# One sum of second weights made in place of its block, and three token-tile pairs instead of one in seven block products in the first unit

## The chip, the cores and the metric

The kernel runs on one core of one Trainium2 chip. The metric is the device time of one execution in microseconds. Engines: PE (TensorE, matmuls), DVE (VectorE), ACT (ScalarE), POOL (GpSimd) and SP (SyncE, which only issues transfers here).

## The reference

```python
def _attn_ref(q, k, v):                       # 8 batches, 12 heads, 448 tokens, 64 wide
    scores = scale * np.matmul(q, k.transpose(0, 1, 3, 2))
    attn = np.maximum(scores, 0.0) ** 2 / S
    return np.matmul(attn, v)
...
def _moe_ref(x, g_ln, w_ch1, w_ch2):          # x: 8 x 448 x 768
    mu = np.mean(x, axis=-1, keepdims=True)
    var = np.mean((x - mu) ** 2, axis=-1, keepdims=True)
    xn = (x - mu) / np.sqrt(var + 1e-06) * g_ln
    ch = np.maximum(xn @ w_ch1, 0.0) @ w_ch2  # 768 x 3072, then 3072 x 768
    return x + ch
```

Attention comes first, its heads are put side by side as x, and x goes through the two layers.

## The kernel before

Inputs and output are float32; what TensorE reads is bfloat16. The eight batches follow one another. In each, q and k of a period (four heads, three periods to a batch, numbered through all batches) are loaded by POOL's queue and transposed by a transfer on SP's queue; scores (L610) go through relu (L619 on ACT, L621 on DVE), a square (L634 on DVE, L636 on POOL) and AV (L676). The result, x transposed, is summed (POOL, L767 to L770), centred (save L874, subtraction L882), and goes through the first layer (L970, L988, or in seven block products L1210) to h, which is held as 24 blocks of 128 by tokens.

**Units and tiles.** The second layer takes two batches as a unit u, whose 896 tokens are seven tiles m of 128. In unit 0, tiles 0 to 2 are batch 0, tiles 4 to 6 are batch 1, and tile 3 has a part of each. h of tiles 0 to 3 lies in h1, that of tiles 4 to 6 in hb. The second weight w2 (24 blocks of 128 x 768) is seen as four quarters, b11 and b12 (upper 12 blocks, left and right 384 columns), b21 and b22 (lower 12 blocks).

**Single tiles** (`ffn_2`, L1535): for each half of the columns, 24 matmuls of 128 x 384 into a bank (four steps of six, L1543) and one evacuation (L1559), which multiplies by the row's factor and adds x.

**Pairs in seven products** (`ffn_w`, L1421): two tiles and the four quarters are a 2 x 2 block product that is done in seven products P1, P2, P6, P5, P7, P3, P4 of 12 matmuls each (two steps of six, L1452), with an evacuation after each (L1460). On the side of the weights they need the sums T3 = b22 + b12, T1 = b12 - b11, T2 = T3 - b11, T4 = b21 - T2 (`make_sum`, L1309; 12 blocks of 128 x 384 each, written at L1320, L1322, L1328, L1330); on the side of h the differences S3, S2, S1, S4 (`s_op`, L1397, two instructions each, L1408), S3, S1 and S4 in place and S2 in a block of its own (`s2_of`).

In unit 0 the tiles 4, 5, 6, 3, 2 are single and (0, 1) is a pair; in the other units tile 2 is single and (0, 1), (3, 4), (5, 6) are pairs. `store_tile` issues two transfers for each piece of output.

**Order.** All instructions are ordered by a planner when the program is built (class `Order`): steps are put on the engine lists with estimated costs; on each engine the step that can start first goes first, then the one with the lower key; steps with two engines are given to the one that ends them sooner and yield to steps of one engine that could start at the same time. `segment` places TensorE's work of a stage: it walks through the stage's steps (`f1_steps` of one batch, then steps of the second layer) and puts pieces of the next batch's attention, the visits, between them when they are due and ready; then the next batch is centred. Hooks at numbered steps add other work: the block sums (`next_sum`, key 5.0), the scaling of w1 by g_ln (`put_gains_on_w1`, L1035 on ACT, L1037 on DVE), the differences of a pair (`pair_start`, key -2.9). Evacuations have key -3.0.

The stage that holds unit 0's second layer is built by the call of `segment` at L1820: the first layer of batch 1 (24 steps of six matmuls), five single tiles (40 steps), one pair (14 steps), with batch 2's attention as visits. `make_w1_sums` and `make_x_sums` place the sums for the first layer of later batches.

Of the kernel before, what the change touches and what calls it, by code (L numbers as in the profile page):

```python
# [202 lines left out]
def kernel(  # L203
# [10 lines left out]
    nc = tc.nc  # L214
    P = 128
# [8 lines left out]
    J = 7  # L224
# [830 lines left out]
    D_FREE = J * hd  # L1055
    T3_HOME = slice(D_FREE + 2 * W_BLOCK, D_FREE + 2 * W_BLOCK + KQ * SH)

    def make_w1_sums(first):

        if first:  # L1060
            places = ([("D", D_FREE + i * W_BLOCK, []) for i in range(2)]
                      + [("B", i * W_BLOCK, [later("s2 used", 0)] if i < 2 else []) for i in (2, 3, 4, 5, 6, 0, 1)])
        else:
            places = ([("C", i * W_BLOCK, [later("qk_done", LAST_B)]) for i in range(7)]
                      + [("D", T3_HOME.start, [later("f1_end", LAST_B - 1)]), ("at", 0, [later("av_done", LAST_B)])])
        b_done = 2 if first else LAST_B - 1

        def home(kind, o):
            t = at_all if kind == "at" else region(kind)
            return t[:, o:o + W_BLOCK].rearrange("p (k c) -> p k c", k=KQ)  # L1070
# [35 lines left out]
    def make_x_sums(b):  # L1106
# [10 lines left out]
        else:  # L1117
            o = x_all[:, 4:6, :].rearrange("p m c -> p (m c)")
            t = {"T1": o[:, :n], "T2": o[:, n:2 * n], "T3": region("D")[:, T3_HOME], "T4": homes["v"][:, 2 * RING * S:2 * RING * S + n]}
# [189 lines left out]
    def make_sum(name, k, o, deps, key):  # L1309
# [5 lines left out]
        prev = {"T1": [], "T3": [], "T2": "T3", "T4": "T2"}[name]  # L1315
# [17 lines left out]
        m = n if prev else 1  # L1333
# [6 lines left out]
    def make_sums(part):  # L1340

        if part == 0:
            v_t = v_pool.tile([P, H // 2, S], bf16, tag="v0")
            c_t = xc_pool.tile([P, K1, S], bf16, tag="xc0")
            v_b, c_b = (blocks(t.rearrange("p a c -> p (a c)"), J) for t in (v_t, c_t))
            x_b = blocks(xT_all[:, 4 * d_model:], 6)
            x_free = [ops[x, bb] for x in ("x_read", "turn_x") for bb in range(2)]
            at_end = blocks(at_all[:, (N_AT - 1) * 2 * S:], 5)
            todo = ([("T3", k, v_b[:, k:k + 2], []) for k in (0, 2, 4)] + [("T3", k, c_b[:, k - 6:k - 4], []) for k in (6, 8, 10)]
                    + [("T1", 7 + k, at_end[:, k:min(k + 2, 5)], [later("av_done", 1)]) for k in (0, 2, 4)] + [  # L1350
                    ("T2", 0, v_b[:, 6:7], []), ("T2", 1, c_b[:, 6:7], []),
                    ("T2", 2, x_b[:, 0:2], x_free), ("T2", 4, x_b[:, 2:4], x_free), ("T2", 6, x_b[:, 4:6], x_free)])
        else:
            a_t = big_pool.tile([P, BIG], bf16, tag="A")
            a_b = blocks(a_t, 14)
            d_b = blocks(region("D"), J)
            gone, turned = [ops["f2_end", 1]], [ops["qk_free", 1]]
            todo = ([("T2", k, a_b[:, k - 8:k - 6], gone) for k in (8, 10)]
                    + [("T1", a, d_b[:, a:z], turned) for a, z in ((0, 2), (2, 4), (4, 6), (6, 7))]
                    + [("T4", k, a_b[:, k + 4:k + 6], gone) for k in (0, 2, 4, 6, 8)]  # L1360
                    + [("T4", 10, blocks(x_all[:, 6, :], 2), [later("m2_out")])])
        sum_queue.extend(todo)
# [9 lines left out]
    def s2_of(u):  # L1372

        return region("B")[:, :KH * P].rearrange("p (k c) -> p k c", c=P) if u == 0 else s2_home
# [22 lines left out]
    def s_op(u, m, name, part, deps):  # L1397

        k = slice(part * KH // 2, (part + 1) * KH // 2)
        k_hi = slice(KH + k.start, KH + k.stop)  # L1400
        a1, a2 = tile_cols(u, m), tile_cols(u, m + 1)
        s2_t = s2_of(u)
        a11, a12, a21, a22 = h1[:, k, a1], h1[:, k_hi, a1], h1[:, k, a2], h1[:, k_hi, a2]
        o, i0, i1 = {"S3": (a21, a21, a11), "S2": (s2_t[:, k], a22, a21), "S1": (a11, a11, s2_t[:, k]),
                     "S4": (a12, a12, s2_t[:, k])}[name]

        def emit(eng):
            (nc.vector if eng == "DVE" else nc.gpsimd).tensor_sub(o, i0, i1)  # L1408
        return R.add("DVE", 570.0, emit, deps, key=-2.9, port=True)
# [11 lines left out]
    def ffn_w(u, m, name, part):  # L1421
# [4 lines left out]
        t1, t2 = (0, 1) if m < 3 else (m - 3, m - 2)  # L1426
# [8 lines left out]
        if final and name == "P4":  # L1435
            last_product(u, m, part, e, r2, deps)
            return
        s2_t = s2_of(u)
# [3 lines left out]
        a = {"P1": lambda k: stat(u, m, k), "P2": lambda k: stat(u, m, KH + k), "P6": lambda k: s2_t[:, k],  # L1442
             "P5": lambda k: stat(u, m, k), "P7": lambda k: stat(u, m + 1, k), "P3": lambda k: stat(u, m, KH + k),
             "P4": lambda k: stat(u, m + 1, KH + k)}[name]
# [12 lines left out]
        def evac(key, tile_n, cols, r, more, deps):  # L1457
            def emit(eng):
                o = e["o", 1 if key in ("p5", "C22") else 0][:, cols]
                nc.vector.scalar_tensor_tensor(o, e["ps", bank], r, o if more else xm[u, m + tile_n][:, cols],  # L1460
# [13 lines left out]
        elif name == "P6":  # L1474
            evac("c2", 0, hi, r1, False, [e["c1"], o_done[e["turn"]][1]])
            s2_last = [op, e["S1"], e["S4"]]
            if m == 3:
# [9 lines left out]
        elif name == "P7":  # L1487
            ev = evac("C22", 1, hi, r2, True, [e["p5"]])
            o_done[1 - e["turn"]][1] = store_tile(u, m + 1, hi, ev, False, e["o", 1])
# [4 lines left out]
        else:  # L1494
# [3 lines left out]
            o_done[e["turn"]][0] = store_tile(u, m + 1, lo, ev, False, e["o", 0])  # L1498
            if m == 3:
                ops["m3_out", u] = e["C12"]  # L1500
            elif m == 5 or u == 0:
                now_known(ev, "f2_out", b)
# [384 lines left out]
```

## Time and profile before

| what | us |
|---|---|
| median of 3 runs | 515.39 (515.30 to 516.42) |
| the profiled execution | 515.06 |
| its span on the core | 513.2 |
| PE / DVE / ACT / POOL busy in the span | 500.2 / 389.9 / 225.6 / 177.7 |
| first layer of batch 1, matmuls | 62 to 96.2 (with the end of batch 0's) |
| unit 0's second layer, with visits | 96.2 to 159.4 |
| first layer of batch 2 starts | 160.0 |

Lines such as L1452 are those of the kernel before. A line of a group gives line, engine, operation, output <- inputs, shape, count and durations. A line of a stretch gives the busy time of each engine in it and, in brackets, the count of instructions. Tiles are named without their numbers: `w` is w1 or w2, `t` and `a_t` are big regions of SBUF, `f_ps` the second layer's banks of PSUM. The granted clock of TensorE is 1.00 throughout.

### The profile page before, as it was taken

The page shows a single profiled execution, that of the slowest core. Times are in us where ns is not written, and L with a number is a line of the kernel's source. Part 1 is how long each engine was busy: PE and PEld are TensorE (multiplying, and loading weights), DVE is VectorE, ACT ScalarE, POOL GpSimd, SP SyncE. Part 2 cuts the span into 40 slices and gives each one's busy share as a digit, 9 for nine tenths or more (in the row PEclk, how much of TensorE's full clock was granted, in tenths as well). Part 3 has the DMA queues.
Part 4 walks back from the last instruction along what each step waited for, and adds up shares of the span by engine and source line. Part 5 has one row for each costly group of instructions (what it writes and reads, how often), then busy time and mean ns, then how long its engine had stood idle before and what let it go on. Part 6 is the DMA issues. An engine that isn't in the chain of part 4 may idle for free.

```text
span 513.2 us, 10746 instructions
## 1 busy us (share of the span) xinstructions
PE 500.2 (97%) x4416; PEld 305.9 (60%) x4416; DVE 389.9 (76%) x732; ACT 225.6 (44%) x351; POOL 177.7 (35%) x205
## 2 busy tenths in 40 slices
PE   5899999999999999999999999999999999999997
PEld 3444455555555445677555775567656675579864
DVE  5988647877986979778778698865888688966843
ACT  5977622652303564156530664236731476115300
POOL 7420500425623066536633067233266033200000
PEclk9999999999999999999999999999999999999999
DMA  9999999789798187797387787894789710123022
GB/s 194 197 188 195 202 202 140 73 104 105 107 145 109 36 86 77 120 157 80 31 119 93 109 79 63 126 128 54 70 84 137 129 21 1 47 63 45 2 63 61
DMA packets 145948, 51.88 MB, mean 101 GB/s; under 512 B 123238, under 2 KB 144108, under 8 KB 145900
## 3 DMA queue, kind: packets, MB, share of 16 engines
q0 software_dynamic: 82224, 25.50, 46.9%
q1 hardware_dynamic: 59036, 18.82, 21.6%
q10 hardware_dynamic: 4640, 6.88, 4.6%
q8 instruction: 34, 0.56, 0.4%
q14 instruction: 14, 0.11, 0.1%
HBM read 51.91 MB, written 11.01 MB: 123 GB/s over the span
## 4 chain that ended last, share of the span: by engine, by line
PE 94%; DVE 3%; ACT 1%; DMA 1%; issue 1%; ACTq 0%; DVEq 0%
PE f_ps L1452 26%; PE f_ps L970 19%; PE f_ps L1543 12%; PE f_ps L1210 10%; PE ps L988 7%; PE sc L610 7%; PE ps L676 5%; PE x_ps L1210 2%; PE y_ps L1210 2%; DVE at_all L634 1%; ACT at_all L619 1%; DVE t L387 1%; DMA f<-in_q_dram 1%; PE ps L532 1%; PE f_ps L950 0%
## 5 line engine op out<-in xcount | busy, mean ns | idle before, releaser
L619 ACT ACTIVATE at_all<-sc 128x896 bf16<-128x896 f32 x120 | 105.4, 925 | 101.1 <-PE sc L610 99.8
L970 PE MATMUL f_ps<-a,w 128*128 128x448 bf16 x516 | 101.5, 353 | 0.0
L634 DVE TENSOR_TENSOR at_all<-at_all 128x896 bf16<-128x896 bf16 x154 | 96.8, 660 | 1.9 <-ACT at_all L619 1.9
L1452 PEld LDWEIGHTS <-h 128*128 128x128 bf16 x708 | 68.4, 98 | 47.3 <-issue 2.8
L442 POOL DMA_DIRECT2D v_t<-in_v_dram x36 | 21.5, 603 | 170.2 <-PE sc L610 145.1
L970 PEld LDWEIGHTS <-w 128*128 128x128 bf16 x516 | 48.9, 98 | 48.8 <-issue 5.5
L1452 PE MATMUL f_ps<-w,h 128*128 128x384 bf16 x360 | 62.8, 326 | 0.0
L423 POOL DMA_DIRECT2D t<-in_k_dram x36 | 55.9, 2137 | 0.0
L423 POOL DMA_DIRECT2D t<-in_q_dram x36 | 42.0, 1340 | 39.5 <-DMA t<-t 28.1
L621 DVE TENSOR_SCALAR at_all<-sc 128x896 bf16<-128x896 f32 x39 | 42.4, 1087 | 15.9 <-PE ps L676 8.7
L999 ACT ACTIVATE h<-f_ps 128x448 bf16<-128x448 f32 (+1 forms) x65 | 32.9, 506 | 47.6 <-PE f_ps L970 46.3
L610 PE MATMUL sc<-t 64*64 64x448 bf16 x672 | 49.5, 367 | 2.9 <-DVE t L387 1.5
L1210 PEld LDWEIGHTS <-w 128*128 128x128 bf16 x432 | 41.0, 98 | 5.8 <-issue 2.7
L988 PE MATMUL ps<-a,w 128*128 128x448 bf16 x186 | 40.2, 352 | 0.0
L1543 PE MATMUL f_ps<-w,h 128*128 128x384 bf16 x240 | 40.0, 326 | 0.0
L1236 DVE CUSTOM_DVE_ANT_0 h<-f_ps,o_all 128x448 bf16<-128x448 f32 x32 | 19.5, 619 | 20.3 <-ACT h L999 6.9
L610 PEld LDWEIGHTS <-t 64*64 64x64 bf16 x672 | 18.4, 107 | 26.3 <-issue 17.9
L1460 DVE SCALAR_TENSOR_TENSOR o_all<-f_ps,r_t,x_all 128x384 f32<-128x384 f32 x39 | 23.9, 613 | 12.0 <-PE f_ps L1452 11.9
L1543 PEld LDWEIGHTS <-h 128*128 128x128 bf16 x240 | 23.3, 98 | 15.8 <-issue 0.6
L1210 PEld LDWEIGHTS <-t 128*128 128x128 bf16 x318 | 30.2, 98 | 4.1 <-issue 1.3
L1460 DVE SCALAR_TENSOR_TENSOR o_all<-f_ps,r_t,o_all 128x384 f32<-128x384 f32 x30 | 18.4, 614 | 16.5 <-PE f_ps L1452 16.5
L385 ACT CAST xT_all<-ps 128x768 bf16<-128x768 f32 (+2 forms) x28 | 17.8, 641 | 28.7 <-PE ps L676 17.7
(158 smaller groups left out, 718.4 us busy)
## 6 DMA issues: line engine op xcount, KB each, us to landing
w<-in_moe_w_ch_dram POOLq DMA_DIRECT2D x4, 1152.0 KB, 39.3
out_dram<-o_all ACTq DMA_DIRECT2D x43, 96.0 KB, 2.7
t<-in_q_dram POOLq DMA_DIRECT2D x36, 112.0 KB, 4.0
t<-in_k_dram POOLq DMA_DIRECT2D x36, 112.0 KB, 5.2
v_t<-in_v_dram POOLq DMA_DIRECT2D x36, 112.0 KB, 3.3
out_dram<-o_all SPq DMA_DIRECT2D x35, 96.0 KB, 2.3
w<-in_moe_w_ch_dram POOLq DMA_DIRECT2D x4, 768.0 KB, 19.0
out_dram<-o_all ACTq DMA_DIRECT2D x13, 192.0 KB, 3.0
```

What stands on the lines that cost most here:

```text
L423: nc.gpsimd.dma_start(qk_stage()[half * T:(half + 1) * T, t].rearrange("p j (h d) -> p j h d", d=D), src[b, h0:h0 + 2].rearrange("h (p j) ...
L610: nc.tensor.matmul(sc[rows_of(half), r, :S], turned[rows_of(r), 1, s, rows_of(half)], turned[rows_of(r), 0, :, rows_of(half)], start=True, ...
L619: nc.scalar.activation(attn[n, s], st[0][:, :, :S], Act.Relu, scale=rc2)
L621: nc.vector.tensor_scalar(attn[n, s], st[0][:, :, :S], rc2, 0.0, op0=Alu.mult, op1=Alu.max)
L634: nc.vector.tensor_mul(attn[n, s], attn[n, s], attn[n, s])
L970: nc.tensor.matmul(st[0], w1[:, ki, ni * P:(ni + 1) * P], xc[b][:, ki, :], start=(i == 0), stop=(i == K1 - 1))
L988: nc.tensor.matmul(st[0], w1[:, ki, ni * P:(ni + 1) * P], xc[b][:, ki, :], start=ki == 0, stop=ki == K1 - 1)
L999: nc.scalar.activation(o, st[0][:, c], Act.Relu)
L1210: nc.tensor.matmul(e["ps", bank][:, n, :], a[:, k, n * P:(n + 1) * P], x[:, k, :], start=name in ("P1", "P2", "P5") and n == 0 and k == 0, ...
L1452: nc.tensor.matmul(e["ps", bank], a(k), w(k), start=new and k == 0, stop=k == KH - 1, skip_group_check=True)
L1460: nc.vector.scalar_tensor_tensor(o, e["ps", bank], r, o if more else xm[u, m + tile_n][:, cols], op0=Alu.mult, op1=Alu.add)
L1543: nc.tensor.matmul(o_st["ps"], stat(u, m, ki), w2[:, ki, j * hd:(j + 1) * hd], start=(ki == 0), stop=(ki == K2 - 1))
```

## The change

- T1 is written over b12 (after T3 has been made from it), not into 12 blocks elsewhere. All sums are queued by one function, two per step from step 13 on. The places of T2 and T4 are others.
- A single tile, which can no longer read b12, is done by way of T1 (`ffn_x`): X = h_up b11 (12 matmuls) is evacuated to the right half with x added; Z = h_up T1 + h_low b22 (24) is added to it; Y = h_low b21 (12) is accumulated on X and evacuated to the left half. Three evacuations in place of two, and two stores in place of one. This holds for tile 2 in all four units.
- In unit 0 the tiles (4, 5) and (6, 3) become pairs in seven products beside (0, 1). The order is: tile 2, (0, 1), (4, 5), (6, 3).
- S2 of unit 0 has another place in two halves; the sums of w1 for the first layer lie in regions A and B, free after pair (6, 3), and partly in C.
- The second of each two stores of unit 0 is issued by SP and not by ACT, as in the other units.

The diff, cut to its core:

```diff
     def make_w1_sums(first):
 
-        if first:
...
+        gone = [ops["f2_end", 1]]
+        places = ([("B", i * W_BLOCK, gone) for i in range(7)] + [("A", i * W_BLOCK, gone) for i in range(7)]
+                  + [("end", W_BLOCK, [later("s2 used", 0)])])
+        n = 3 * G_STEADY
+        places = places[:n] if first else (
+            places[n:] + [("C", i * W_BLOCK, [later("qk_done", LAST_B)]) for i in range(7)] + [("at", 0, [later("av_done", LAST_B)])])
...
-            t = {"T1": o[:, :n], "T2": o[:, n:2 * n], "T3": region("D")[:, T3_HOME], "T4": homes["v"][:, 2 * RING * S:2 * RING * S + n]}
+            t = {"T1": o[:, :n], "T2": o[:, n:2 * n], "T3": x_all[:, 6, :n], "T4": homes["v"][:, 2 * RING * S:2 * RING * S + n]}
...
-        prev = {"T1": [], "T3": [], "T2": "T3", "T4": "T2"}[name]
+        prev = {"T1": "T3", "T3": None, "T2": "T3", "T4": "T2"}[name]
...
-    def make_sums(part):
...
+    AT_END = at_all[:, (N_AT - 1) * 2 * S:]
+
+    def make_sums():
...
+        d_b, d_free = blocks(region("D"), 14), [ops["qk_free", 1]]
+        sum_queue.extend(
+            [("T3", k, v_b[:, k:k + 2], []) for k in (0, 2, 4)] + [("T3", k, c_b[:, k - 6:k - 4], []) for k in (6, 8, 10)]
+            + [("T1", k, b12[:, k:k + 2], []) for k in range(0, KH, 2)]
+            + [("T2", 0, v_b[:, 6:7], []), ("T2", 1, c_b[:, 6:7], [])]
+            + [("T2", k, x_b[:, k - 2:k], x_free) for k in (2, 4, 6)]
+            + [("T2", k, d_b[:, k - 8:k - 6], d_free) for k in (8, 10)]
+            + [("T4", k, d_b[:, k + 4:k + 6], d_free) for k in (0, 2, 4, 6, 8)]
+            + [("T4", 10, blocks(AT_END, 2), [later("av_done", 1)])])
...
-    def s2_of(u):
-
-        return region("B")[:, :KH * P].rearrange("p (k c) -> p k c", c=P) if u == 0 else s2_home
+    def s2_of(u, part):
+
+        if u == 0:
+            t = AT_END[:, W_BLOCK:2 * W_BLOCK] if part else homes["v"][:, 2 * RING * S:2 * RING * S + W_BLOCK]
+            return t.rearrange("p (k c) -> p k c", c=P)
+        return s2_home[:, part * KH // 2:(part + 1) * KH // 2]
+
+    def partner(u, m):
+        return 3 if (u, m) == (0, 6) else m + 1
+
+    def h_block(u, m, upper, part):
+
+        k = slice(part * KH // 2, (part + 1) * KH // 2)
+        if u == 0 and m > 3:
+            return hb[upper][:, k, (m - 4) * P:(m - 3) * P]
+        return h1[:, upper * KH + k.start:upper * KH + k.stop, tile_cols(u, m)]
...
-        k = slice(part * KH // 2, (part + 1) * KH // 2)
-        k_hi = slice(KH + k.start, KH + k.stop)
-        a1, a2 = tile_cols(u, m), tile_cols(u, m + 1)
-        s2_t = s2_of(u)
-        a11, a12, a21, a22 = h1[:, k, a1], h1[:, k_hi, a1], h1[:, k, a2], h1[:, k_hi, a2]
-        o, i0, i1 = {"S3": (a21, a21, a11), "S2": (s2_t[:, k], a22, a21), "S1": (a11, a11, s2_t[:, k]),
-                     "S4": (a12, a12, s2_t[:, k])}[name]
+        s2_t = s2_of(u, part)
+        a11, a12, a21, a22 = (h_block(u, t, upper, part) for t in (m, partner(u, m)) for upper in range(2))
+        o, i0, i1 = {"S3": (a21, a21, a11), "S2": (s2_t, a22, a21), "S1": (a11, a11, s2_t), "S4": (a12, a12, s2_t)}[name]
...
+            if u == 0 and m < 6:
+                now_known(s2_last, "s2_free", 0, 4 if m == 0 else 6)
+            elif m == 3:
...
-            if m == 3:
-                ops["m3_out", u] = e["C12"]
-            elif m == 5 or u == 0:
+            o_done[e["turn"]][0] = store_tile(u, m2, lo, ev, False, e["o", 0])
+            if 3 in (m, m2):
+                ops["m3_out", u] = e["C12"] if m == 3 else ev
+            if (u, m) == (0, 6):
+                ops["f2_end", 1] = op
+            if m in (5, 6) or (u, m) == (0, 0):
...
-    def f2_deps(u, m, j, part, parts):
...
-    def ffn_2(u, m, j, part, parts):
...
+    def fx_deps(u, m, name, part):
+
+        b = 2 * u
+        e = xs.get((u, m), {})
+        a, z = part * KH // 2, (part + 1) * KH // 2
+        if name == "X":
+            return [h_of(b, a, z), min(f_banks, key=when), ops["w2", K2 - 1]]
+        if name == "Z" and part < 2:
+            return [h_of(b, a, z), e["z0"], ops["sums", "T1"]]
+        return [h_of(b, KH, K2)] + ([e["x hi"]] if name == "Y" else [])
+
+    xs = {}
+
+    def ffn_x(u, m, name, part):
+
+        b = 2 * u
+        e = xs.setdefault((u, m), {})
+        deps = fx_deps(u, m, name, part)
+        if name == "X" and part == 0:
+            if when(f_banks[0]) > when(f_banks[1]):
+                f_banks.reverse()
+                f_tags.reverse()
+            e["z0"] = f_banks[1]
+            e["turn"] = o_take()
+        w = b21 if name == "Y" else b11 if name == "X" else b12 if part < 2 else b22
+        upper = name == "Y" or part > 1
+
         def emit(eng):
-            if part == 0:
+            if name in "XZ" and part == 0:
                 o_ps = f_tile([P, hd], fp32)
-                o_st["ps"] = o_ps
-            for ki in range(part * K2 // parts, (part + 1) * K2 // parts):
-                nc.tensor.matmul(o_st["ps"], stat(u, m, ki), w2[:, ki, j * hd:(j + 1) * hd],
-                                 start=(ki == 0), stop=(ki == K2 - 1))
-        op = R.pe(975.0 * 4 / parts, emit, f2_deps(u, m, j, part, parts))
-        if (u, m) == (0, 6) and j == 1 and part == parts - 1:
-            ops["f2_end", 1] = op
-        if part < parts - 1:
-            return
-        ps = o_st["ps"]
-        ri = m if m < 3 else m - 3
-
-        if j == 0:
-            o_st[u, m] = o_take()
-        turn = o_st[u, m]
-
-        def evac(eng):
-            cols = slice(j * hd, (j + 1) * hd)
-            nc.vector.scalar_tensor_tensor(o_all[:, turn, cols], ps, rstd[b][:, ri:ri + 1], xm[u, m][:, cols],
-                                           op0=Alu.mult, op1=Alu.add)
-        ev = R.add("DVE", 620.0, evac, [op, ops["rstd", b], o_done[turn][j]], key=-3.0)
-        f_use(ev)
-        if j == 1:
-            if (u, m) == (0, 2):
+                e["ps", name] = o_ps
+            ps = e["ps", "Z" if name == "Z" else "X"]
+            for i in range(KH // 2):
+                k = part % 2 * KH // 2 + i
+                nc.tensor.matmul(ps, stat(u, m, upper * KH + k), w[:, k], start=name in "XZ" and part == 0 and i == 0,
+                                 stop=name != "Z" and k == KH - 1 or part == 3 and k == KH - 1, skip_group_check=True)
+        op = R.pe(975.0, emit, deps)
+        lo, hi = slice(0, hd), slice(hd, d_model)
+        r, o = rstd[b][:, m:m + 1], o_all[:, e["turn"]]
+
+        def evac(key, bank, cols, more, deps):
+            def emit(eng):
+                nc.vector.scalar_tensor_tensor(o[:, cols], e["ps", bank], r, o[:, cols] if more else xm[u, m][:, cols],
+                                               op0=Alu.mult, op1=Alu.add)
+            e[key] = R.add("DVE", 620.0, emit, [op, ops["rstd", b]] + deps, key=-3.0)
+            return e[key]
+        if (name, part) == ("X", 1):
+            evac("x hi", "X", hi, False, [o_done[e["turn"]][1]])
+        elif (name, part) == ("Z", 3):
+            o_done[e["turn"]][1] = store_tile(u, m, hi, evac("hi", "Z", hi, True, [e["x hi"]]), False, o)
+        elif (name, part) == ("Y", 1):
+            ev = evac("lo", "X", lo, False, [o_done[e["turn"]][0]])
+            o_done[e["turn"]][0] = store_tile(u, m, lo, ev, False, o)
+            f_banks[:] = [e["hi"], ev]
+            f_tags.reverse()
+            if u == 0:
                 now_known(ev, "m2_out")
-            elif m in (2, 6):
+            else:
                 now_known(ev, "f2_out", b)
...
-            sto = R.add("SP" if r and u > 0 else "ACT", 550.0, store, [ev], key=-0.5, load=(T, 150.0))
+            sto = R.add("SP" if r else "ACT", 550.0, store, [ev], key=-0.5, load=(T, 150.0))
...
+    def fx_steps(u):
+        return [("fx", u, 2, name, p) for name, n in (("X", 2), ("Z", 4), ("Y", 2)) for p in range(n)]
...
-        def first_pair():
-            now_known(ops["f2_end", 1], "s2_free", 0, 0)
-            pair_start(0, 0)
-        segment(f1_steps(1) + f2_steps(0, (4, 5, 6, 3, 2)) + fw_steps(0, [0]), vis, 2, 9000.0,
-                hooks=[(K2 // 2, lambda: make_sums(0))]
-                + [(i, next_sum) for i in range(K2 // 2 + 1, K2 + 6 * PARTS, SUM_EVERY)] + [(K2, put_gains_on_w1), (K2 + 6 * PARTS, lambda: make_sums(1)),
-                       (K2 + 8 * PARTS, first_pair)]
-                + [(i, next_sum) for i in range(K2 + 6 * PARTS + 1, K2 + 10 * PARTS + 2)])
+        now_known(later("av_done", 1), "s2_free", 0, 0)
+        n_x, n_w = len(fx_steps(0)), len(fw_steps(0, [0]))
+        segment(f1_steps(1) + fx_steps(0) + fw_steps(0, [0, 4, 6]), vis, 2, 9000.0,
+                hooks=[(K2 // 2, make_sums)] + [(K2 // 2 + 1 + i // 2, next_sum) for i in range(30)]
+                + [(K2, put_gains_on_w1), (K2, lambda: pair_start(0, 0)), (K2 + n_x, lambda: pair_start(0, 4)),
+                   (K2 + n_x + n_w, lambda: pair_start(0, 6))])
...
-            f2 = fw_steps(u, [0]) + f2_steps(u, [2]) if b % 2 == 0 else fw_steps(u, [3, 5])
+            f2 = fw_steps(u, [0]) + fx_steps(u) if b % 2 == 0 else fw_steps(u, [3, 5])
```

## The prediction

> **What bounds the kernel now.** I read the page's busy times and chain first, then the waits, then the stretch of time that the change touches, engine by engine.
>
> ```profile
> PE 500.2 (97%) x4416; PEld 305.9 (60%) x4416; DVE 389.9 (76%) x732; ACT 225.6 (44%) x351; POOL 177.7 (35%) x205
> ...
> PE 94%; DVE 3%; ACT 1%; DMA 1%; issue 1%; ACTq 0%; DVEq 0%
> ```
>
> Busy times, then the chain that ended last by engine: TensorE's matmuls are 94% of the path. The view of who waited for whom, cut to TensorE, has 8 rows that come to 8.9 us; all belong to attention or the start, and no row is of the second matmul. What TensorE does less of there is on the path.
>
> The change works between the end of the second batch's first matmul (96.2 us) and the start of the third batch's (160.0 us), and just ahead. Busy time by stretch (length, then PE, PEld, DVE, ACT, POOL, granted clock, DMA share, GB/s):
>
> ```profile
> 83.40:96.20 12.80, 12.80 (x70) 6.59 (x69) 10.76 (x31) 4.45 (x15) 4.67 (x4) 1.00 0.94 101
> 96.20:160.00 63.80, 63.71 (x507) 35.70 (x505) 52.92 (x106) 22.90 (x28) 27.81 (x32) 1.00 0.83 112
> 136.00:146.00 10.00, 10.00 (x82) 5.74 (x80) 9.84 (x25) 0.50 (x1) 4.74 (x5) 1.00 0.86 88
> ```
>
> TensorE is full in all three, VectorE 83% full in the stage, and in the third row 98% full with TensorE still full: a nearly full VectorE did not hold TensorE up. ACT has 40.9 us free in the stage.
>
> The chain in order of time (start, length, what):
>
> ```profile
> 106.27 7.96 PE f_ps L1543 x48
> ...
> 151.57 7.80 PE f_ps L1452 x48
> 159.37 0.69 PE sc L610 x12
> 160.06 5.78 PE f_ps L970 x30
> ...
> 211.20 7.80 PE f_ps L1543 x48
> ```
>
> 48 matmuls of a single tile (L1543) take 7.80 us at 211.20, 48 of a seven-product pair (L1452) 7.80 us at 151.57: 162.5 ns each in either form. At 106.27 the 48 took 0.16 us more: a pause lies among them.
>
> **The change, part by part.**
>
> *Matmuls.* A single tile takes 48, a pair in seven products 84 instead of 96. The first unit had five single tiles and a pair, 5 x 48 + 84 = 324; it gets one single tile and three pairs, 48 + 3 x 84 = 300. 24 x 162.5 ns = 3.90 us off TensorE in the stage. Tile 2 of each unit keeps 12 + 24 + 12 = 48 in its new order (X, Z, Y): nothing.
>
> *VectorE, added.* Rows of one line's instructions (ns min/median/max, first and last start):
>
> ```profile
> L1408 DVE TENSOR_TENSOR h<-h x20: 540/550/558, 137.5 to 473.0; 128x768 bf16<-128x768 bf16 x20
> L1460 DVE SCALAR_TENSOR_TENSOR o_all<-f_ps,r_t,x_all x39: 603/616/619, 147.5 to 503.6; 128x384 f32<-128x384 f32 x39
> ```
>
> Two new pairs make 8 differences each: 16 x 0.55 = 8.8 us. Evacuations: two pairs have 14 where four tiles had 8, and the one single tile 3 where it had 2: 7 x 0.616 = 4.3 us. The block sums are as many as before (12 blocks of each of four), T1 in place at the same price (0.55 us for two blocks, L1322). If nothing else moved, the stage would hold 52.9 + 8.8 + 4.3 = 66.0 us of VectorE in 63.8 - 3.9 = 59.9 us.
>
> What can leave it. Block sums that fell after 96.2 (L1322 3.1, L1328 3.0, L1330 3.4 us, by stretch and line) are queued two per step from step 13, so some go into the 12.80 - 10.76 = 2.0 us that VectorE had free from 83.4 on; I count 2.0. Scaling w1 (8 on VectorE, 4.7 us, L1037) and relu (6, 5.5 us, L621) may go to ACT, at 1.58 us (L1035) and 0.92 us (L619) each: 18 us for ACT, which has 40.9 - 3.9 = 37 free. 66.0 - 2.0 - 4.7 - 5.5 = 53.8 of 59.9 us, 90%, under the 98% of the third row above. So I price the added VectorE work at nothing; its cover is gone when more than 6.1 us of these 12.2 us stay. Later units get one more evacuation each (0.62 us), in stages where VectorE is 75 to 82% full: nothing.
>
> *The sum behind the single tile.* Z reads T1, which needs all of T3 (6 instructions) and then 6 of its own. VectorE in order of time:
>
> ```profile
> 83.38 1.01 DVE L1320 TENSOR_TENSOR v_t<-w 128x768 bf16<-128x768 bf16 x2
> ...
> 90.69 1.26 DVE L1322 TENSOR_TENSOR at_all<-w 128x768 bf16<-128x768 bf16 x3
> 92.99 0.23 DVE L1001 TENSOR_SCALAR h<-f_ps 128x64 bf16<-128x64 f32 x1 [1.03 <-PE f_ps L970]
> ...
> 132.12 1.66 DVE L1322 TENSOR_TENSOR t<-w 128x768 bf16<-128x768 bf16 x1
> ...
> 154.45 1.42 DVE L882 TENSOR_TENSOR a<-xT_all,sum_t 128x768 bf16<-128x768 bf16 x2
> ```
>
> Five of T1's twelve blocks were ready at 92.0; the other seven are 4 x 0.55 = 2.2 us more, so about 94.2, while Z starts at 96.2 + 12 x 0.1625 = 98.2. Cover 4 us. X now wants the whole second weight; the first sum at 83.38 already read its last rows, so it has landed. A pair's seven products wait for T2, T3, T4: T2's remainder (about 3 us) runs beside the single tile's 7.8 us and the pair's first 3.9. Between none and 1 us of TensorE may be lost here, as the queue holds statistics (4.7 us from 95.86 to 102.5) too; I take 0, since in all later pairs (708 matmuls of L1452) no row shows a wait.
>
> *The port.* The sum at 132.12 took 1.66 us where its like takes 0.55, while POOL added (0.93 us at 132.43, 1.12 at 133.44). One stretch of 1.1 us is what I allow for the 16 new differences; it fits the 6.1 us spare. The Trainium skill, SBUF — State Buffer, section "SBUF: two separate sides", says that a VectorE instruction with two SBUF inputs and a GpSimd instruction that reads SBUF exclude each other for the whole instruction. By that rule, estimated, all 7.0 us of POOL's adds in this stage could become VectorE's: 60.8 of 59.9 us, and 0.9 us lost.
>
> *Stores.* The first unit's were 18, all issued by ACT; now 28, half of them on SP. ACT issues 14 x 0.50 us instead of 18; a relu behind a store waits there for the store's evacuation, as it does now. On SP 14 x 0.47 us stand in the queue with the transposes that bring q and k. A store waits there for its evacuation and holds the next transpose; the transpose issued at 97.33 was used by the scores at 114.2, so some 12 us lie between. Nothing, unless a store stood there that long.
>
> *Homes of sums and of later weight sums.* The s2 blocks, T4 and the w1 sums only change places. The w1 sums now wait for the last pair's end (before 160), where the first of them was made at 162.5: nothing. Six of the last batch's nine no longer wait for its scores; no TensorE wait stood on them: nothing.
>
> **The sum.** Span 513.2 - 3.9 = 509.3; the profiled run of 515.06 has 1.86 around its span: 511.2; the median of the runs is 0.33 above the profiled run: **511.5 us**.
>
> **Rivals.**
>
> *The attention of batch 2 sets the stage's end.* The last step ahead of its first matmul, the centring (154.45 + 1.42), ended at 155.87, the old stage at 160.0. With 3.9 us off, the stage wants to end at 156.1, so the margin is 0.2 us if attention doesn't move at all. Against it: its last AV (143.98) followed squares that VectorE made at 142.60 to 144.28, behind 4 differences and 10 block sums from 137.51 on; the sums are earlier in the new order, so it may move up. For it: VectorE picks evacuations, differences and sums ahead of squares. Each us that this chain slips is a us lost: between 0.2 and 3.9 us, 512 to 515.4. Mostly about 2 us, 513.5. Chance 0.18.
>
> *VectorE becomes the bound (the slower side).* If the flexible work stays where it is, the stage cannot be shorter than 66.0 us against 63.8: 2.2 us slower, 517.6. It decides from 6.1 us of unmoved work on; at all 12.2 us unmoved it is the full price. For it: the planner gives an either-engine step to VectorE whenever that ends it sooner by its estimate (L1037: 0.5 against 1.48 us), and put 8 of 12 there. Against it: the same comparison counts the queue on VectorE, and steps bound to VectorE go first. Chance 0.14.
>
> *The single tile or first pair waits for its own sums.* T1, T2 or T4 late by more than their 4 us of cover, TensorE idle until they come: 1 to 3 us, 512.5 to 514.5, and as much as 516.5 if each pair repeats it. Chance 0.04.
>
> **How the numbers follow.** Forecast 0.64 with 510.8 to 512.4 (0.7 less if pauses around the removed tiles go too, such as the 0.16 us above; 0.9 more by small waits); 0.18, 0.14 and 0.04 for the rivals. About 0.2% (1.0 us) is what a measurement of this kernel can tell from no change. Faster by more: 0.64 + 0.12 + 0.02 = 0.78. Slower by more: 0.12 of the VectorE case + 0.01 = 0.13. Between: 0.06 + 0.02 + 0.01 = 0.09. The range 510.8 to 515.2 holds the forecast, nearly all of the attention case and the small ends of the others, 0.81 or so.
>
> **What would show it.** Right: the first batch-2 matmul of the first layer (160.0) starts near 156.1, TensorE has no wait for VectorE in the stage, scaling and relu are mostly on ACT there, L1408 has 24 instructions there in place of 8, and all later stages keep their lengths. Wrong: rows of TensorE waiting for L1408, L1460 or the block sums; a centring that ends after TensorE's last product; VectorE over 97% full for the whole stage with TensorE pausing; or later stages that lengthen by what the first one won.

## The result

| | median, us | runs | ratio to before |
|---|---|---|---|
| before | 515.75 | 515.30 to 516.42 (4) | 1 |
| after | 512.48 | 512.14 to 513.47 (4) | 0.9939 [0.992, 0.9957] |

The changed kernel is 3.2 us faster (2.2 to 4.1 by the interval); 511.5 had been forecast from a before of 515.39; a fourth run of before has since moved its median to 515.75. The profiled execution took 513.47 us with a span of 511.7. Lines have moved by a few numbers: the pairs' matmuls are L1454 (before L1452), the single tile's L1567 (L1543), differences L1410 (L1408), evacuations L1462 (L1460), stores L1602, the sums of second weights L1318 (T3), L1320 (T1), L1326 (T2) and L1328 (T4). Kernels of the experiments shift them by a few more.

Busy times and the chain by engine, from the page of after:

```profile
PE 496.6 (97%) x4392; PEld 303.5 (59%) x4392; DVE 393.1 (77%) x740; ACT 236.8 (46%) x368; POOL 175.5 (34%) x205
...
PE 86%; DVE 8%; DMA 3%; ACT 2%; issue 1%; SPq 0%; ACTq 0%; DVEq 0%
```

4416 - 4392 = 24 matmuls are gone and 3.6 us of TensorE's busy time. The chain has more of VectorE than before, but that is no loss by itself: the chain follows whatever came last, and where two engines arrive together it names either. The waits tell whether TensorE stood still.

The stage of unit 0's second layer in the chain of after (start, length, what), from its first single-tile matmul to the first layer of batch 2:

```profile
97.42 2.92 PE f_ps L1567 x18
...
151.66 4.87 PE f_ps L1454 x30
156.53 0.69 PE sc L610 x12
157.22 0.90 PE f_ps L970 x5
158.12 7.87 DMA x_all<-xT_all
```

It is 157.22 - 97.42 = 59.80 us long; before it was 160.06 - 96.36 = 63.70. That is 3.90 us less, the term of the sum to the hundredth. This execution entered the stage 1.06 us later than the profiled one of before, as its first transfers of q and k came later; another execution of the same kernel (below) did not, so spans should not be subtracted without that. Stage lengths by the same landmarks, us:

| | unit 0's second layer | from there to unit 1's single tile | unit 1 to unit 2 | unit 2 to unit 3 | rest |
|---|---|---|---|---|---|
| before | 63.70 | 51.14 | 119.90 | 119.03 | 63.07 |
| after | 59.80 | 52.00 | 120.20 | 119.26 | 63.02 |

So -3.90 + 0.86 + 0.30 + 0.23 - 0.05 = -2.56, and with the 1.06 at the start the span falls from 513.2 to 511.7.

Busy time in the stage (length, PE, PEld, DVE, ACT, POOL, clock, DMA share, GB/s):

```profile
97.25:157.15 59.90, 59.77 (x482) 33.36 (x480) 53.62 (x110) 32.45 (x37) 24.26 (x28) 1.00 0.81 104
```

TensorE has 0.13 us of pauses in the whole stage, VectorE 53.62 us of work against 53.8 forecast, and ACT took 9.5 us more than before (22.90).

What gave back part of it is in who waited for whom, cut to TensorE; two rows are new:

```profile
PE f_ps L970 <- DVE h L1001: 0.7, 1, 0.7
PE f_ps L1208 <- ACT o_all L385: 0.5, 1, 0.5
```

The first lies at 171.73, in the first layer of batch 2. Going back from it through VectorE and SP's queue, in order of time (in brackets the idle time before an instruction and what ended it):

```profile
156.25 1.77 SPq L1602 DMA_DIRECT2D out_dram<-o_all  x2
158.12 3.10 SPq L797 DMA_TRANSPOSE x_all<-xT_all  x1
```

```profile
166.01 0.56 DVE L822 BATCH_NORM_STATS2 st<-x_all 128x6 f32<-128x384 bf16 x1 [1.36 <-DMA x_all<-xT_all]
```

The transposes that give batch 2's x by tokens (L797) were issued at 146.53 before and at 158.12 now, behind the last pair's stores. VectorE's statistics stood idle for them, and an evacuation of the first layer behind the statistics came late. In the program, batch 2's turn for its x is let go by the last second-layer evacuation of batch 1. That was tile 6's, in the middle of the stage; it is now the pair (6, 3)'s, at its end.

### The profile page after: what moved, and what is told of

It reads as the page before. It is cut to its first block, busy times and chain, and to the rows that moved or that the text cites. A ratio compares the mean times of both kernels' runs of the same rounds, so it can differ in the third digit from the quotient of the medians.

```text
span 511.7 us, 10775 instructions
## 1 busy us (share of the span) xinstructions
PE 496.6 (97%) x4392; PEld 303.5 (59%) x4392; DVE 393.1 (77%) x740; ACT 236.8 (46%) x368; POOL 175.5 (34%) x205
## 4 chain that ended last, share of the span: by engine, by line
PE 86%; DVE 8%; DMA 3%; ACT 2%; issue 1%; SPq 0%; ACTq 0%; DVEq 0%
PE f_ps L1454 29%; PE f_ps L970 17%; PE f_ps L1208 9%; PE ps L988 6%; PE f_ps L1567 6%; PE sc L610 6%; PE ps L676 5%; DVE at_all L634 2%; PE x_ps L1208 2%; PE y_ps L1208 2%; DMA x_all<-xT_all 2%; DMA f<-in_k_dram 1%; ACT at_all L619 1%; DVE o_all L1462 1%; DVE h L1410 1%
## 5 line engine op out<-in xcount | busy, mean ns | idle before, releaser
L970 PE MATMUL f_ps<-a,w 128*128 128x448 bf16 x510 | 100.9, 353 | 0.8 <-DVE h L1001 0.7
L1454 PEld LDWEIGHTS <-h 128*128 128x128 bf16 x732 | 71.0, 98 | 48.4 <-issue 1.9
L634 DVE TENSOR_TENSOR at_all<-at_all 128x896 bf16<-128x896 bf16 x154 | 95.3, 653 | 1.9 <-ACT at_all L619 1.8
L1454 PE MATMUL f_ps<-w,h 128*128 128x384 bf16 x480 | 84.4, 326 | 0.0
L970 PEld LDWEIGHTS <-w 128*128 128x128 bf16 x510 | 48.2, 98 | 49.6 <-issue 7.4
L621 DVE TENSOR_SCALAR at_all<-sc 128x896 bf16<-128x896 f32 x40 | 43.5, 1088 | 16.5 <-PE ps L676 10.2
L988 PE MATMUL ps<-a,w 128*128 128x448 bf16 x192 | 41.5, 352 | 0.0
L1462 DVE SCALAR_TENSOR_TENSOR o_all<-f_ps,r_t,x_all 128x384 f32<-128x384 f32 x47 | 28.8, 613 | 10.9 <-PE f_ps L1454 10.7
L1462 DVE SCALAR_TENSOR_TENSOR o_all<-f_ps,r_t,o_all 128x384 f32<-128x384 f32 x36 | 22.1, 614 | 17.1 <-PE f_ps L1454 17.1
L1567 PE MATMUL f_ps<-w,h 128*128 128x384 bf16 x192 | 32.4, 326 | 0.0
L385 ACT CAST xT_all<-ps 128x768 bf16<-128x768 f32 (+2 forms) x31 | 19.1, 623 | 24.5 <-PE ps L676 23.8
L676 PE MATMUL ps<-at_all,v_t 64*64 64x448 bf16 x552 | 29.8, 350 | 0.0
```

Of the source, the lines that this page charges most:

```text
L621: nc.vector.tensor_scalar(attn[n, s], st[0][:, :, :S], rc2, 0.0, op0=Alu.mult, op1=Alu.max)
L634: nc.vector.tensor_mul(attn[n, s], attn[n, s], attn[n, s])
L676: nc.tensor.matmul(av_st[n][half][rows_of(hh)], (v_slot(n)[rows_of(half), hh] if b > 1 else vt[b][rows_of(half), 2 * pn + hh])[:, s * D:(s ...
L970: nc.tensor.matmul(st[0], w1[:, ki, ni * P:(ni + 1) * P], xc[b][:, ki, :], start=(i == 0), stop=(i == K1 - 1))
L988: nc.tensor.matmul(st[0], w1[:, ki, ni * P:(ni + 1) * P], xc[b][:, ki, :], start=ki == 0, stop=ki == K1 - 1)
L1454: nc.tensor.matmul(e["ps", bank], a(k), w(k), start=new and k == 0, stop=k == KH - 1, skip_group_check=True)
```

## The experiments

Three questions: is it the matmuls that gave the time; what took 0.7 us back; and how near was the changed kernel to the slower cases.

### The changed kernel once more

> The changed kernel itself, beside the others on the same chip: 0.994 of before, 3.2 us less, as measured; its stage 59.9 us and the wait of TensorE for L1001 in the next one again, if it belongs to the order and not to one execution.

512.57 us (511.70 to 513.37, 6 runs), 0.9934 [0.9917, 0.9951], span 509.9. The stage is 59.81 us and begins where it did before (96.33); the four stages are 59.81, 51.30, 120.21 and 119.26. There is no row of L970 waiting for L1001 here, and the second stage lost 0.16 us, not 0.86. SP issued the transposes at 157.02, 0.9 us after the stage's end as in the profiled execution; they landed 7.2 us after issue instead of 7.9, and VectorE stood 0.67 us for them instead of 1.36. The wait is real but varies from one execution to the next; the lengthening of units 1 and 2 does not.

### Batch 2's x let go earlier

In the last pair, the third evacuation (that of P6, the last one that adds tile 6's x) gives the turn, and the last one no longer does:

```diff
-            evac("c2", 0, hi, r1, False, [e["c1"], o_done[e["turn"]][1]])
+            ev = evac("c2", 0, hi, r1, False, [e["c1"], o_done[e["turn"]][1]])
+            if (u, m) == (0, 6):
+                now_known(ev, "f2_out", b)
...
-            if m in (5, 6) or (u, m) == (0, 0):
+            if m == 5 or (u, m) == (0, 0):
```

> The changed kernel, but the planner lets batch 2's x transposes overwrite tiles 4 to 6's x as soon as pair (6, 3) has evacuated tile 6 (after P6), not at the pair's end. Theory W (the 0.87 us that the first layer of batch 2 lost are this wait): transposes issued before 153 instead of 158.1, no wait of TensorE for L1001 there, that stage 51.2 us instead of 52.1, time 0.8 us under the changed kernel, about 511.7. Rival S (the transposes were late because stores now stand before them on SP's queue, or because loads crowd the transfers): still a wait of 0.5 us or more, time within 0.2 us of the changed kernel. Rival T (the loss is the planner's noise): stage anywhere, no clear change.

512.09 us (511.55 to 514.31, 6 runs), 0.9931 [0.991, 0.9952], span 509.8. SP's queue:

```profile
148.17 3.68 SPq L797 DMA_TRANSPOSE x_all<-xT_all  x1
```

The second stage is back at 51.14 us, as before the change, and the wait for L1001 is gone; the first stage stays at 59.80. So the later release, through the order that the planner makes of it, is what cost 0.16 to 0.86 us. (In the two kernels of the next section, which issue these transposes earlier too, that stage is 51.13 us.) Against the changed kernel the gain of about 0.4 us lies inside the intervals: the traces show it, the times do not settle it.

### Two pairs, and one

Tiles 6 and 3 single in the new form, by way of T1 (order 2, (0, 1), (4, 5), 6, 3); then 4, 5, 6 and 3 all single, so that only the new form and the changed homes remain:

```diff
-        segment(f1_steps(1) + fx_steps(0) + fw_steps(0, [0, 4, 6]), vis, 2, 9000.0,
+        segment(f1_steps(1) + fx_steps(0) + fw_steps(0, [0, 4]) + fx_steps(0, (6, 3)), vis, 2, 9000.0,
```

> The changed kernel with tiles 6 and 3 single (by way of T1) after pairs (0, 1) and (4, 5): 12 matmuls more. Theory M (TensorE's matmul count sets the stage): stage 59.9 + 1.95 = 61.85 us; 1.95 us slower than the changed kernel there, but the x transposes come earlier, so 0.8 of it returns in the next stage: about 513.6. Rival O (the gain came from the earlier sums and the order, not the count): stage near 59.9, time at 512.5 or below.

> The changed kernel with only pair (0, 1); tiles 2, 4, 5, 6, 3 are single by way of T1: the in-place sum and the new order alone, with the 324 matmuls of before. Theory M: stage 63.8 us as before, time within 0.5 us of before (515.4), five more evacuations unseen. Rival O: stage near 60 us, time 512 to 513. Rival V (the way through T1 costs TensorE something in waits that the pairs hid): over 516.

| pairs in unit 0 | median, us | runs | ratio | stage, us |
|---|---|---|---|---|
| three (changed) | 512.57 | 511.70 to 513.37 (6) | 0.9934 [0.9917, 0.9951] | 59.81 |
| two | 514.21 | 513.91 to 515.12 (9) | 0.9971 [0.9957, 0.9984] | 62.28 |
| one | 516.36 | 516.28 to 517.30 (12) | 1.0016 [1.0005, 1.0027] | 64.66 |

Each pair taken back adds 2.47 and 2.38 us to the stage, of which 12 x 0.1625 = 1.95 us are its matmuls. The rest of the change, with one pair, is no gain: its stage is 64.66 us against 63.70 before. The pairs earn all of it.

Theory M was right about what sets the stage and low in both sizes (61.85 and 63.8 us forecast), and the one-pair kernel came out over 516, the number of rival V. Its waits are not on the way through T1, though. They are rows of attention; with one pair:

```profile
PE sc L610 <- DVE at_all L621: 0.6, 1, 0.6
...
PE slot L861 <- POOL rsum_t L770: 0.3, 1, 0.3
```

Both lie in the stage (at 119.86 and 147.64) and make up its 0.92 us of pauses. With two pairs only the second is there, 0.33 us. With three pairs there is neither; why fewer pairs bring them stays open.

### The stores on ACT again

```diff
-            sto = R.add("SP" if r else "ACT", 550.0, store, [ev], key=-0.5, load=(T, 150.0))
+            sto = R.add("SP" if r and u > 0 else "ACT", 550.0, store, [ev], key=-0.5, load=(T, 150.0))
```

> The changed kernel with all stores of unit 0 on ACT's queue as before. Theory W (the x transposes of batch 2 wait for pair (6, 3), not for SP's queue): transposes issued within 1 us of where the changed kernel issues them (0.9 us after the stage's end), stages of 59.8 and 51.3 to 52.0 us, time within 0.5 us of the changed kernel. Rival S (the two stores ahead of them on SP are what delays them): issued over 1 us sooner, the first layer of batch 2 back at 51.1.

513.16 us (512.97 to 513.32, 6 runs), 0.9949 [0.9933, 0.9964]; this interval and the changed kernel's overlap, so what follows rests on the trace. The stage is 60.79 us, 1.0 longer, with rows of TensorE waiting that neither execution of the changed kernel has:

```profile
PE sc L610 <- DVE at_all L621: 0.4, 1, 0.4
...
PE f_ps L1454 <- DVE o_all L1462: 0.4, 1, 0.4
```

Two things follow. The move of stores to SP, priced at nothing, is worth about 1 us in the stage (the waits add up to 0.8); that relu on ACT stands behind stores is what I take to be the reason, but in this stage only the waits are shown. (In the next one the chain shows it: issue of a store on ACT's queue until 157.83, relu, square, and TensorE waiting 0.17 us at 162.65.) And with fewer stores ahead of them on SP, the transposes for batch 2's x were issued at 153.52, before the pair's last evacuation at 156.54: what held them on the chip was SP's queue, in the order that the planner wrote, not a semaphore of the pair. That was rival S's sign, over 1 us sooner; its stage of 51.1 us did not come with it: the next stage took 51.55.

### Single tile ahead of the pair in the later units

The lengthening of units 1 and 2 might come from the order pair, then single tile. On top of the earlier release:

```diff
-            f2 = fw_steps(u, [0]) + fx_steps(u) if b % 2 == 0 else fw_steps(u, [3, 5])
+            f2 = fx_steps(u) + fw_steps(u, [0]) if b % 2 == 0 else fw_steps(u, [3, 5])
```

> The kernel with early x transposes, and in units 1 to 3 the single tile ahead of pair (0, 1), as in unit 0. Theory E (the 0.30 and 0.23 us that the stages of units 1 and 2 lost come from the single tile's later evacuations just ahead of the next first layer): those stages back at 119.9 and 119.0 us, time 0.5 us under the kernel with early transposes. Rival: the pair's own end has as many evacuations, so those stages stay at 120.2 and 119.3 or grow.

512.03 us (511.57 to 514.26, 6 runs), 0.9934 [0.9914, 0.9953], against 512.09 without it: no change, the last pairs' matmuls start at 479.68 us against 479.66, and TensorE still waits 0.5 us for ACT's copy (L385). That theory falls. In unit 1 this wait accounts for the loss: it is 0.47 us at 229.24 in the profiled execution, and TensorE's pauses in that stage grew from 0.14 to 0.47 us. In unit 2 no wait stands for the 0.23 us; TensorE is busy 0.19 us longer there. Every kernel with the new single tile has these 0.3 and 0.23 us, so they come from something that those share, such as the tile's third evacuation and second store, T1's home, or the homes of the w1 sums. Which of them, stays open.

### VectorE loaded on purpose

The forecast's slower rival was VectorE as the bound. Each S2 difference of the pairs (4, 5) and (6, 3) was written five times, then nine times (16 and 32 added instructions of 0.55 us, at the rank of the pairs' own differences):

```diff
+        if u == 0 and m > 0:
+            for again in range(4):
+                for part in range(2):
+                    s_op(u, m, "S2", part, [e["S2"][part]])
```

> The changed kernel with each S2 of pairs (4, 5) and (6, 3) written five times instead of once: 16 more VectorE instructions of 0.55 us, 8.8 us, as many as the change added. Its stage has 59.9 us and 53.6 busy on VectorE, with some 5 us of it (relu, scaling) that ACT could take. Theory M (TensorE sets the stage, VectorE has about 6 us to spare and 5 to move): 62.4 less what moves, so no more than 2.5 us lost, most likely 0.5 to 2. Rival V (VectorE already decides): nearly the whole 8.8 us lost.

> The same with each of these S2 written nine times: 32 more, 17.6 us. Theory M: 53.6 + 17.6 - 5 = 66 us of VectorE in the stage, so 6 us lost or somewhat more, since in the two pairs alone (some 32 us of TensorE) the load is higher than in the whole stage. Rival V: 17 us lost. Rival N (added differences are hidden however many): nothing lost.

16 added: 526.87 us (526.08 to 527.66, 4 runs), 1.022 [1.0195, 1.0244]. 32 added: 531.52 (531.22 to 531.88, 4 runs), 1.0305 [1.0285, 1.0325]. All theories missed: 8.8 us of work cost over 14 us, and the next 8.8 only 4.7 (rival V, with 17 us for all 17.6, came nearest to the 19 of the second). Waits of TensorE with 16 added, then busy time by stretch (columns as above):

```profile
PE slot L861 <- POOL rsum_t L770: 5.3, 1, 5.3
...
PE f_ps L970 <- DVE a L882: 4.4, 1, 4.4
```

```profile
154.00:157.00 3.00, 1.47 (x20) 0.51 (x13) 1.86 (x4) 0.63 (x1) 0.41 (x1) 1.00 0.89 183
157.00:160.00 3.00, 0.00 (x0) 0.00 (x0) 0.00 (x0) 0.34 (x2) 2.92 (x5) 0.94 0.75 88
160.00:163.00 3.00, 1.40 (x13) 0.59 (x13) 0.00 (x0) 0.83 (x2) 2.45 (x5) 0.50 1.32 215
```

VectorE did nothing from 157 to 163 us, while TensorE stood from 156.3 to 161.6. What came last is batch 2's attention, the chain squares, attention product, sums of x on POOL, centring (L882). The squares had stood behind the added instructions: the first attention product of the stage came at 136.70 us, against 121.22 in the changed kernel.

### The same load, first or last in rank

Three kernels tell the amount of work on VectorE from its place. They add subtractions of 128 x 384 whose result nobody reads, queued when the pairs (4, 5) and (6, 3) begin: 26 ranked behind all else, the same 26 ranked first, and 8 ranked first.

```diff
+        if u == 0 and m > 0:
+            o = AT_END[:, 2 * W_BLOCK:2 * W_BLOCK + hd]
+            for i in range(13):
+                R.add("DVE", 360.0, lambda eng, o=o: nc.vector.tensor_sub(o, b21[:, 0], b22[:, 0]),
+                      [later("av_done", 1)], key=6.0, port=True)
```

(The other two have `key=-2.9`, and the last has `range(4)`.)

> Added to the changed kernel: 26 subtractions of 128x384 on VectorE whose result nobody reads (13 queued when each of the pairs (4,5) and (6,3) of unit 0 begins; 26 x 0.344 us = 8.9 us by the own sums' row), ranked behind everything else that VectorE has ready, so that squares, relus and evacuations go first. Theory 'chain': what can make the stage late is not VectorE's sum of work but the order on it, since the chain squares of batch 2, attention product, sums of x, centring ends within 0.2 us of TensorE's last product; with the additions ranked last the loss is 0 to 1.0 us. Theory 'capacity': VectorE was busy 53.6 of 59.9 us, so 8.9 us more exceed its idle time by 2.6 us, and the loss is about 2.6 us.

> The same 26 subtractions at the same two places, but ranked ahead of everything else that VectorE has ready (at the rank of the pairs' own differences). Theory 'chain': the squares of batch 2 stand behind them, so the attention products, the sums of x and the centring come later by most of the 8.9 us: loss 5 to 10 us, with VectorE idle while TensorE waits for the centring (L882). Theory 'capacity': as with the yielding ones, about 2.6 us.

> Eight of the subtractions (four at each of the two pairs, 8 x 0.344 us = 2.75 us), ranked ahead of everything else. Theory 'chain': the chain has 0 to 0.2 us to spare, so the loss is 1 to 3 us and shows as a wait for the centring or for the sums of x. Theory 'capacity': 2.75 us fit into the 6.3 us in which VectorE idles, and the loss is under 0.5 us.

These stages are from the first L1572 or L1567 to the first L970 in the timeline; before has 63.81 by it, after 59.90. The changed kernel stands at 0.9939 x 515.81 = 512.66 us beside these runs of before (515.81).

| added | ranked | median, us | runs | ratio | over changed, us | stage, us |
|---|---|---|---|---|---|---|
| 26 (8.9 us) | last | 514.45 | 514.14 to 515.98 (10) | 0.9967 [0.9953, 0.998] | 1.8 | 62.52 |
| 8 (2.75 us) | first | 518.31 | 517.44 to 519.62 (10) | 1.004 [1.0024, 1.0056] | 5.6 | 65.44 |
| 26 (8.9 us) | first | 527.59 | 526.41 to 528.59 (4) | 1.0215 [1.0175, 1.0255] | 14.9 | 75.26 |

Less than a third of the work, put first, costs three times as much as all of it put last (twice as much by the stages). With the 26 ranked last, VectorE is busy 58.88 of the same 59.90 us (97.25 to 157.15); with the 8 ranked first it is busy 52.05, less than in the changed kernel. Where VectorE has time to spare, then, order decides and not the amount, and theory 'capacity' falls with the 8: under 0.5 us forecast, 5.6 measured. Theory 'chain' named the right waits there and was low in size (1 to 3 us, and 5 to 10 for the 26 ranked first). With the 26 ranked last it is the other way round: 'chain' forecast 0 to 1.0 us, 'capacity' 2.6, and the stage is 2.62 us longer. How 2.75 us become 5.6 is seen where batch 2's first attention product of this stage stands on TensorE, in the changed kernel and then with the 8 ranked first:

```profile
121.22 1.49 PE L676 MATMUL ps<-at_all,v_t 64*64 64x448 bf16 x28
```

```profile
127.95 1.49 PE L676 MATMUL ps<-at_all,v_t 64*64 64x448 bf16 x28
```

The first square moved from 114.80 to 116.59 us, the product by 6.7: as I read it, the planner, which puts visits only between pieces of TensorE's list, found it late for its place and gave it a later one. TensorE finished its second-layer products at 156.2, as early as in the changed kernel (156.5); but the sums of x were ready for it only then (L861 at 156.03 against 151.3), the centring ran from 157.95 to 162.5, and TensorE stood for it:

```profile
PE f_ps L970 <- DVE a L882: 2.8, 1, 2.8
```

Part of that wait is not the slot. One of the four subtractions of the centring took 2.40 us, where the longest in the changed kernel takes 0.96, and POOL was making a square beside it:

```profile
157.86 1.67 POOL L636 TENSOR_TENSOR at_all<-at_all 128x896 bf16<-128x896 bf16 x1 [0.84 <-ACT at_all L619]
```

```profile
L882 DVE TENSOR_TENSOR a<-xT_all,sum_t x4: 546/946/2403, 157.9 to 162.0; 128x768 bf16<-128x768 bf16 x3, 128x384 bf16<-128x384 bf16 x1
```

So some 1.4 of the 5.6 us belong to this meeting, by these rows. POOL has a square at this place in two other kernels, with the 26 ranked first and with the 16 added writes, and there too a subtraction is slow (2.26 and 3.96 us). With the 26 ranked last and with the 32 writes it has none, and the longest is 0.96. No run takes the square away alone.

The loss of the yielding ones has the size that capacity gives, and VectorE was nearly full over the whole stage (61.50 of 62.52 us):

```profile
97.96:160.48 62.52, 60.29 (x483) 33.44 (x482) 61.50 (x131) 34.05 (x38) 24.80 (x28) 1.00 0.76 100
```

It reaches TensorE through waits of 1.18, 0.70 and 0.15 us. The longest is for an evacuation that stood behind seven of the added instructions, VectorE first and TensorE after it:

```profile
146.77 3.89 DVE L1425 TENSOR_TENSOR at_all<-w 128x384 bf16<-128x384 bf16 x7
```

```profile
151.25 1.95 PE L1459 MATMUL f_ps<-w,t 128*128 128x384 bf16 x11 [1.18 <-DVE o_all L1467]
```

Seven of them take 7 x 0.357 = 2.5 us elsewhere. The 1.4 us more fall where POOL added: one subtraction took 0.952 us, the last began at 149.72 and the evacuation behind it only at 150.59, and POOL's add at 149.41 took 2.00 us where its like took 0.92.

## Why the prediction was right, point by point

- **Matmuls, 3.90 us.** Right, and shown from both sides: 24 fewer, a stage 3.90 us shorter in one execution of the changed kernel and 3.89 in another, and 2.4 to 2.5 us given back with each pair, of which 1.95 are matmuls and most of the rest waits of attention that only the kernels with fewer pairs have.
- **VectorE, 53.8 of 59.9 us.** The total was right (53.62), its parts were not. Block sums left the stage by 4.8 us instead of 2.0 (9.5 to 4.76); scaling by 2.3 instead of 4.7 (three of twelve stayed on VectorE); relu by 2.2 instead of 5.5 (four stayed). That is 9.2 us instead of 12.2. Most of the other 3 came from rows that the sum had kept as they were: the 16 differences added 7.9 us of busy time instead of 8.8 (12.18 against 4.24 before), the squares took 1.0 less (12.46 against 13.42) and the casts L387 0.6 less. That the total came out is luck.
- **"Its cover is gone when more than 6.1 us stay".** Wrong as a point of decision. 8.9 us more, ranked last, cost 1.8 us (2.62 in the stage, about what lies over the spare 6.3); 2.75 us ranked first, well inside the spare time, cost 5.6. The bound that lies nearest is the attention of batch 2, the first rival; the sum of VectorE's work, the second, binds only behind it.
- **The first rival's margin of 0.2 us.** Its arithmetic held, its loss did not come: the centring's last instruction ran from 155.92 to 156.47, TensorE's last product of the stage ended at 156.53 (by the timeline and the chain of after), and scores stood between that and the first layer. Its first attention product moved from 114.56 to 121.22 (5.6 us later from the stage's start), later and not earlier as I thought possible; it had that much room, and 0.75 us were left before the next first layer at 157.22. The case's range starts at 511.7 by its own terms (511.5 + 0.2), not 512.
- **The single tile's own sums.** Right: the last of T1 ended at 91.78 + 1.47 = 93.25 (94.2 forecast; this execution runs some 1 us late), and no row of TensorE waits for a sum. T2 and T4 were partly made by 95.4. The 708 that the forecast leaned on are weight loads from h (a row of L1452), not matmuls of later pairs; those nine pairs have 9 x 84 = 756. That no row of theirs shows a wait stands.
- **The port.** I allowed 1.1 us for the 16 new differences; they needed none, since they hardly met POOL. All 24 differences in the stage took 0.540 to 0.555 us, and only the one at 149.58 ran beside an add of POOL's, which then took 0.69 us (at 149.96) where its shape took 0.31. Another instruction paid: a scaling of w1 (L1037) beside POOL's adds from 124.27 on took 1.27 us, where the two others took 0.62. The price worked out from the Trainium skill's rule (SBUF — State Buffer, "SBUF: two separate sides"), 0.9 us lost, did not come. The rule itself is not contradicted: where a subtraction of the centring met POOL's square it took 2.40 us, as shown above, and TensorE waited for the centring. What failed in that estimate was to take all of POOL's time as VectorE's.
- **Stores: "nothing, unless a store stood there that long".** Wrong on both sides. The move is worth about 1 us in the stage by the trace, and stores on SP do hold transposes, though not those that the prediction looked at (q and k) but those of x behind them.
- **"All later stages keep their lengths".** This is the step that failed, and nearly all of the gap between 3.9 forecast and 3.2 measured: 0.16 to 0.86 us for the late transposes of x, shown by taking them back; and 0.53 us in units 1 and 2, present in every kernel with the new single tile: in unit 1 a wait for ACT's copy, the cause behind it and that of unit 2 open. The prediction listed what waits for the last pair's end (the w1 sums) and left out what the old single tile 6 had let go in mid-stage.

## What to carry to other kernels

When work is reordered, list what the old order released early, for every name that another step waits on, and not only what the new order needs; a release that moves from the middle to the end of a stage costs in the next stage. When an engine is nearly full, do not ask how many us still fit but what stands behind each added instruction: work that yields is cheap until the engine is full, while a little work ahead of a step that feeds the next stage costs more than its length, since the step it delays may miss its slot (here 2.75 us cost 5.6). A pair or tile moved to fewer matmuls is worth its matmuls' time only while the other chain into the next stage still ends in time; here that chain was within some tenths of a us.

## What was not expected of the hardware

A stop of a few us costs TensorE twice. With 16 added writes TensorE had no matmul from 157 to 160 us, and the granted clock was 0.94 in that stretch and 0.50 in the four stretches of 3 us from 160 to 172, back at 1.00 in that from 175. With the 8 subtractions ranked first it was busy 0.40 of the 3 us from 159 on, and then had 0.62 and 0.81 before full clock. The Trainium skill (TensorE: Matmul & The Clock Gate, "What's actually happening") says that the clock falls to half after an idle window of about 3.4 us and returns after a busy one; the rows agree with the half, and the 2.8 us wait of the second case, with idle time around it, was already enough. In the 3 us from 165 on, at 0.81, 14 matmuls are recorded, against 18 in the next 3 us at full clock. For a stage that ends in such a wait, the loss is the wait and the slow matmuls after it.
